# Sliding-window attention and MLP in one kernel: both halves of a block's scores in one run of matmuls, the second half in the PSUM banks that held an older block's values

## The chip, the cores and the metric

The kernel runs on one core of one Trainium2 chip. The metric is the device time of one launch in microseconds (us); lower is better. Times are given as the median of several runs, and everything that is read from a profile comes from one profiled execution.

## The reference

Two layers follow each other. The first is causal attention over a sliding window of 128 tokens, with a distance bias that differs by head (8 batches, 8 heads, 576 tokens, head size 64). The second is a layer norm with a gain, an MLP of 512 to 2048 to 512 with a ReLU, and a residual.

```python
scores = scale * np.matmul(q, k.transpose(0, 1, 3, 2))          # scale = 1/8
mask = (rel >= 0) & (rel < 128)                                 # rel = query - key
scores = np.where(mask, scores - slopes * np.abs(rel), -1e9)
attn = np.exp(scores - max); attn = attn / (sum + 1e-9)
x = np.matmul(attn, v)                                          # (8, 576, 512) after merging heads
xn = (x - mean) / sqrt(var + 1e-6) * g_ln
out = x + np.maximum(xn @ w_ch1, 0.0) @ w_ch2
```

The kernel leaves out the maximum: it takes exp(scale * scores) and multiplies it with exp(bias), which is zero outside the window.

## The kernel before, in words

**Blocks.** Batches are taken in pairs (p = 0 to 3). A pair has 9 blocks: blocks 0 to 7 hold 128 queries of one of the two batches, and block 8 (T) holds the last 64 tokens of both. That makes 36 blocks, numbered n = 9p + blk. An MLP group g takes 2 blocks (g = 0 to 3) or 4 blocks (g = 4 to 10).

**Attention of one block.** `attend` (L469) computes the scores of some heads with keys on the partitions: 64x64 tiles of the array, four of them beside each other (two halves of the keys by two heads). A block from 2 on has two halves of 4 heads each and so two calls of `attend`; a block 0 or 1 has one call with all 8 heads over its own keys, and T has two calls over the older keys and one (`tail_attend`) over its own. Each call issues 16 matmuls at L495 into one tile `ps_sc` of two PSUM banks, and one exp on ScalarE (L504) from there into `probs` in SBUF. `seen` (L443) lists which parts of the 64x128 score tiles can be seen through the window at all; from the ninth block on only those are computed (half of the matmuls have 64 columns, the others 128). `masks` (L513) multiplies `probs` by exp(bias) on VectorE (L516). `values_at_once` (L571) multiplies the weights with the values into the other tile, `ps_sc[0]` (matmuls at L579), and VectorE takes the result out with a reciprocal of the sums (L587) and a scaled copy (L588). `centre` (L602) subtracts the mean (L616, L620) and has the block turned by DMA. `square` (L661) computes the variance on ScalarE (L664).

**Steps.** For n from 8 on, a loop (L772 to L794) writes four steps for each n: the first has the loads, the values of block n, `centre`, and the first half of the scores of block n + 2; the second has the second half of these scores; the third has the mask of the first half, `square` and DMA transposes of later q and k; the fourth has the mask of the second half. Both halves go through `ps_sc[1]`, so `ps_sc[0]` is the values' alone. Where block n + 1 is a T, the two calls are T's own keys and the next pair's block 0 (n = 16, 25); for n = 8, 17, 26 and 34 there is one call alone. So 23 of the n have two calls.

**Order.** The order on all five engines is written by hand. `weave_at` (L1230) runs an MLP group's matmuls in units and, after unit u, emits the next steps whose place is u. The first MLP product (`mlp1`, L822) has 16 units of four 128x512 matmuls (L832) for a group of four blocks; each unit's ReLU goes to ScalarE (L848), and those of units 6 and 13 to VectorE (L840). The second (`mlp2_seven`, L1049) is a 2x2 block product in seven products instead of eight, each of 16 matmuls of 256 columns (L1062) and so four units, with an addition to the output on VectorE after each (L1083, two instructions). It needs sums of quarters of the hidden layer; `sum_hidden` (L1030, VectorE, L882) computes them during `mlp1` at the units of `SUMS_AT` (L48): after unit 11 three sums of parts 0 to 2 of each half, after unit 14 three of parts 3 to 5, after unit 15 three of parts 6 and 7. The sums after unit 11 need the ReLU of unit 10, those after unit 15 that of unit 15. Where both stand at one unit, the sums are emitted ahead of the steps.

The places of the steps stand in `TWICE` and `LEAD` (L795 to L797): for a group from g = 5 on, steps at units 4, 6, 8, 9 and 11, 13, 15, 15 of `mlp1`, and at 3, 7, 11, 15 and 19, 23, 27, 27 of `mlp2_seven`; g = 4 has 2, 4, 5, 6, then 7, 9, 9, 10, then 12, 14, 14 and, in `mlp2_seven`, 3 ahead of the eight others.

## Time and profile before

| | before |
|---|---|
| median of 3 runs | 308.04 us (307.87 to 308.59) |
| the profiled execution's own time | 307.95 us |
| its span in the profile | 306.2 us |
| granted TensorE clock, mean | 0.993 |
| busy: PE (matmuls) | 296.9 us |
| busy: DVE (VectorE) | 242.8 us |
| busy: ACT (ScalarE) | 181.7 us |
| busy: POOL (GpSimd, here only DMA issue) | 112.3 us |
| exps at L504, 128x1024 | 1.02 us each |
| masks at L516, 128x1024 | 0.68 us each |
| scaled copy of values at L588 | 0.69 us each |

The span is the time between the first and the last instruction of the profile; the 1.75 us between it and the execution's own time lie around it. Matmuls are pipelined, so the duration of one is longer than its share of the time: what counts is the distance between the starts. A row of the timeline gives the start, the time covered, the engine, the line, the shapes and, in brackets, for how long the engine sat idle before it and what ended that.

### The profile page before, as it was taken

To read this page: it belongs to the slowest core of one execution; us is meant where nothing else is said; L and a number is where in the kernel's file an instruction comes from. 1 tells how busy PE (TensorE), PEld (TensorE's weight loads), DVE (VectorE), ACT (ScalarE), POOL (GpSimd) and SP (SyncE) were. 2 spreads that over 40 slices of the span, in tenths; PEclk is the share of its full clock that TensorE was granted. 3 is DMA by queue.
4 is the path that set the end of the run, shared out by engine and by line. 5 is a ranking of instruction groups with operands and counts; after the bars stand their busy time and mean duration, and the time that the engine had idled before them with its cause. 6 is when DMAs were issued, how large, how long until landed. Compare 5 with 4: busy or idle time off the path is not lost.

```text
span 306.2 us, 9262 instructions
## 1 busy us (share of the span) xinstructions
PE 296.9 (97%) x3778; PEld 203.2 (66%) x3778; DVE 242.8 (79%) x646; ACT 181.7 (59%) x332; POOL 112.3 (37%) x153
## 2 busy tenths in 40 slices
PE   6899999999999999999999999999999999999994
PEld 2477755866755568646864686568656865698883
DVE  2588878779996799569967986798799878978983
ACT  5588776768966863675368635853586268506500
POOL 8933659763774372475107250760000000000000
PEclk9799999999999999999999999999999999999999
DMA  9999999999999999999999999999451043005014
GB/s 98 172 202 200 194 158 170 205 135 89 138 126 186 146 132 145 181 184 148 112 171 120 125 121 149 119 151 120 105 122 37 19 96 77 19 19 137 3 34 103
DMA packets 150074, 38.03 MB, mean 124 GB/s; under 512 B 140656, under 2 KB 145920, under 8 KB 150032
## 3 DMA queue, kind: packets, MB, share of 16 engines
q0 software_dynamic: 103792, 18.46, 96.0%
q1 hardware_dynamic: 45760, 18.60, 37.1%
q8 instruction: 29, 0.48, 0.7%
q10 hardware_dynamic: 480, 0.39, 0.5%
q14 instruction: 13, 0.11, 0.2%
HBM read 36.90 MB, written 9.44 MB: 151 GB/s over the span
## 4 chain that ended last, share of the span: by engine, by line
PE 91%; DMA 4%; ACT 1%; DVE 1%; POOL 1%; issue 1%; DVEq 0%; ACTq 0%; POOLq 0%
PE ps_m L832 35%; PE ps_s L1062 25%; PE ps_m L862 9%; PE ps_sc L495 6%; PE ps_sc L579 5%; PE ps_q L1141 4%; PE ps_x L956 3%; DMA q<-q 3%; DMA first<-in_k_dram 2%; PE ps_tr L343 1%; PE ps_warm L331 1%; POOL first L187 1%; PE ps_pv L550 1%; PE ps_tx L640 1%; PE ps_t L956 1%
## 5 line engine op out<-in xcount | busy, mean ns | idle before, releaser
L832 PE MATMUL ps_m<-xT,w1g 128*128 128x512 f16 (+1 forms) x512 | 103.7, 353 | 0.1
L848 ACT ACTIVATE ht_all<-ps_m 128x512 f16<-128x512 f32 (+1 forms) x143 | 71.5, 512 | 26.1 <-PE ps_m L832 24.0
L504 ACT ACTIVATE probs<-ps_sc 128x1024 f16<-128x1024 f32 x56 | 56.6, 1024 | 45.4 <-PE ps_sc L495 45.4
L832 PEld LDWEIGHTS <-w1g 128*128 128x128 f16 x512 | 47.7, 98 | 42.6 <-issue 0.3
L286 POOL DMA_DIRECT2D vx<-in_v_dram x40 | 34.1, 859 | 67.9 <-PE ps_sc L579 38.1
L1062 PE MATMUL ps_s<-w,s 128*128 128x256 f16 x384 | 43.8, 273 | 0.0
L1062 PEld LDWEIGHTS <-s 128*128 128x128 f16 x384 | 36.7, 98 | 4.7
L516 DVE TENSOR_TENSOR probs<-probs,m 128x1024 f16<-128x1024 f16 x56 | 36.9, 683 | 2.5 <-ACT probs L504 2.5
L1062 PE MATMUL ps_s<-w,ht_all 128*128 128x256 f16 x288 | 34.3, 273 | 0.0
L862 PE MATMUL ps_m<-w,ht_all 128*128 128x512 f16 x128 | 31.3, 380 | 0.0
L1062 PEld LDWEIGHTS <-ht_all 128*128 128x128 f16 x288 | 27.4, 98 | 4.9
L275 POOL DMA_DIRECT2D q<-in_q_dram x40 | 27.4, 697 | 6.0 <-DMA vx<-in_v_dram 2.2
L1083 DVE SCALAR_TENSOR_TENSOR o<-ps_s,rstd,x 128x256 f32<-128x256 f32 x48 | 21.0, 478 | 8.5 <-PE ps_s L1062 8.4
L882 DVE TENSOR_TENSOR s<-ht_all 128x1024 f16<-128x1024 f16 (+2 forms) x36 | 20.5, 571 | 7.9 <-ACT ht_all L848 6.7
L495 PE MATMUL ps_sc<-q,k 64*64 64x128 f16 (+1 forms) x1088 | 24.8, 212 | 0.6 <-ACT q L436 0.3
L495 PEld LDWEIGHTS <-k 64*64 64x64 f16 x1088 | 16.2, 108 | 13.2 <-issue 10.3
L588 DVE SCALAR_TENSOR_TENSOR x<-ps_sc,rec 128x512 f16<-128x512 f32 x32 | 22.1, 691 | 1.1
L272 POOL DMA_DIRECT2D k<-in_k_dram x20 | 17.9, 910 | 8.4 <-DMA k<-k 5.9
L664 ACT ACTIVATE junk<-xc 128x512 f16<-128x512 f16 x28 | 17.6, 628 | 5.7 <-DVE xc L620 5.6
L1083 DVE SCALAR_TENSOR_TENSOR o<-ps_s,rstd,o 128x256 f32<-128x256 f32 x36 | 15.7, 478 | 3.4 <-PE ps_s L1062 3.1
L579 PEld LDWEIGHTS <-probs 128*128 128x128 f16 x384 | 15.9, 98 | 3.6
L862 PEld LDWEIGHTS <-ht_all 128*128 128x128 f16 x128 | 11.1, 98 | 10.8
(117 smaller groups left out, 371.7 us busy)
## 6 DMA issues: line engine op xcount, KB each, us to landing
out_dram<-o SPq DMA_DIRECT2D x64, 128.0 KB, 2.5
vx<-in_v_dram POOLq DMA_DIRECT2D x32, 128.0 KB, 7.1
w<-in_moe_w_ch_dram POOLq DMA_DIRECT2D x8, 512.0 KB, 11.2
k<-in_k_dram POOLq DMA_DIRECT2D x30, 128.0 KB, 7.2
q<-in_q_dram POOLq DMA_DIRECT2D x48, 64.0 KB, 6.7
q<-in_q_dram POOLq DMA_DIRECT2D x10, 128.0 KB, 6.8
out_dram<-o SPq DMA_DIRECT2D x10, 64.0 KB, 1.9
k<-in_k_dram POOLq DMA_DIRECT2D x8, 64.0 KB, 7.7
```

Source lines behind the costliest of these rows:

```text
L275: nc.gpsimd.dma_start(out=t[half, b], in_=tokens.rearrange("h (c r) d -> r c h d", r=2)[r],)
L286: nc.gpsimd.dma_start(out=vx[p0 : p0 + n, :, 0:D], in_=v[b, :, t0 : t0 + n, :].rearrange("h p d -> p h d"),)
L495: nc.tensor.matmul(in_halves(ps[cols, j, n, t, :])[:, r, queries], kt[rows, hp, cols], in_halves(qt[rows, b, hp])[:, r, queries], start=no ...
L504: nc.scalar.activation(out=dst.rearrange("p (n j) q -> p j n q", j=2), in_=ps.rearrange("p j n t q -> p j n (t q)"), func=AF.Exp, scale=in ...
L516: nc.vector.tensor_tensor(out=dst, in0=dst, in1=mask, op=ALU.mult)
L579: nc.tensor.matmul(ps[:, h, 0 : D + 1], pr[:, h, t, :], vext[(p * NSLOT + o) % NV][:, h, :], start=(n == 0), stop=(n == len(terms) - 1),)
L588: nc.vector.scalar_tensor_tensor(out=x.rearrange("p (h d) -> p h d", h=H), in0=ps[:, :, 0:D], scalar=1.0, in1=rec.unsqueeze(2).broadcast_t ...
L832: nc.tensor.matmul(ps[:, 0:cols], w[:, kb, fb * P : (fb + 1) * P], xT[:, kb, 0:cols], start=(kb == 0), stop=(kb == NKB - 1),)
L848: nc.scalar.activation(out=ht[:, fb, :], in_=ps[:, 0:cols], func=AF.Relu)
L862: nc.tensor.matmul(sums[at], ht[:, fb, at * P : (at + 1) * P], w2[:, fb, :], start=(fb == 0), stop=(fb == NFB - 1),)
L1062: nc.tensor.matmul(ps[:, pair, :], lhs[:, fb, at : at + P], rhs[:, fb, :], start=(first and pair == 0 and fb == 0), stop=(fb == half - 1), ...
L1083: nc.vector.scalar_tensor_tensor(out=outs[at][:, cols], in0=ps[:, pair], scalar=rstd[:, n : n + 1], in1=(xs[p, blk] if fresh else outs[at] ...
```

## The change

The first half's `attend` moves from the first step into the second, so that the 32 matmuls of the two halves follow each other. The first half stays in `ps_sc[1]`; the second goes to `ps_sc[0]`, where the values of block n are. What lies there outside the visible parts is old, so `seen` gives the whole tiles for these calls. The second half's exp is not emitted with its matmuls but in the third step (`exps`), and both masks stand in the fourth. The places are changed: the third step comes at unit 7 instead of 8, 14 instead of 15, and 9 instead of 11, the fourth at 13 instead of 15; the second step of the last quarter at 22 instead of 23 and the third at 24 instead of 27.

```diff
-    def seen(p, blk, o, t):
+    def seen(p, blk, o, t, all_of_it):
...
-        if p == 0 and blk < SEEN:
+        if all_of_it or p == 0 and blk < SEEN:
             return [(0, both, every), (1, both, every)]
...
-    def attend(p, blk, keys, mask, tag, hps, sc=None):
+    def attend(p, blk, keys, mask, tag, hps, sc=None, put_off=False):
...
-                for c, r, queries in seen(p, blk, o, t):
+                for c, r, queries in seen(p, blk, o, t, sc == 0):
...
-        nc.scalar.activation(
-            out=dst.rearrange("p (n j) q -> p j n q", j=2),
-            in_=ps.rearrange("p j n t q -> p j n (t q)"),
-            func=AF.Exp,
-            scale=inv_sqrt_d,
-        )
+
+        def weights():
+            nc.scalar.activation(
+                out=dst.rearrange("p (n j) q -> p j n q", j=2),
+                in_=ps.rearrange("p j n t q -> p j n (t q)"),
+                func=AF.Exp,
+                scale=inv_sqrt_d,
+            )
+
+        if put_off:
+            scored_only.append(weights)
+        else:
+            weights()
...
+    def exps():
+
+        while scored_only:
+            scored_only.pop()()
...
         step += [(centre,) + order[n]]
-        step += [(attend, *args, 1) for args in todo[:1]]
-        second = [(attend, *args, 1) for args in todo[1:]]
-        third = [(masks, *args[:2], 1) for args in todo[:1]] + [(square, n)]
+
+        second = [(attend, *args, sc, sc == 0) for args, sc in zip(todo, (1, 0))]
+        third = [(exps,), (square, n)]
...
-        fourth = [(masks, *args[:2], 1) for args in todo[1:]]
+        fourth = [(masks, *args[:2], 1) for args in todo]
...
-    TWICE = [4, 6, 8, 9, 11, 13, 15, 15], [3, 7, 11, 15, 19, 23, 27, 27]
-    LEAD = [([2, 4, 5, 6, 7, 9, 9, 10, 12, 14, 14], [3] + TWICE[1])]
+    TWICE = [4, 6, 7, 9, 11, 13, 14, 15], [3, 7, 9, 13, 19, 22, 24, 27]
+    LEAD = [([2, 4, 5, 6, 7, 9, 9, 10, 12, 14, 15], [3] + TWICE[1])]
```

More of the change, by code (lines that the diff above doesn't have):

```diff
@@ L436, in copy_second @@
             copy(out=dst, in_=ps[b][:, 0 if t is q else 1])
-    weights_of, unmasked, scored = {}, {}, []
+    weights_of, unmasked, scored, scored_only = {}, {}, [], []
     def in_halves(t):
         return t if len(t.shape) == 3 else t.rearrange("p (r c) -> p r c", r=2)
-    def seen(p, blk, o, t):
+    def seen(p, blk, o, t, all_of_it):
         both, every = slice(0, 2), slice(0, HALF)
         first, second = slice(0, HALF // 2), slice(HALF // 2, HALF)
-        if p == 0 and blk < SEEN:
+        if all_of_it or p == 0 and blk < SEEN:
             return [(0, both, every), (1, both, every)]
```

## The prediction, as it was put on record

> **What bounds the kernel now.** I read the page's busy times first, then its chain of work that ended last, then the timelines of PE, DVE and ACT around the scores.

> ```profile
> PE 296.9 (97%) x3778; PEld 203.2 (66%) x3778; DVE 242.8 (79%) x646; ACT 181.7 (59%) x332; POOL 112.3 (37%) x153
> ```
> ```profile
> PE 91%; DMA 4%; ACT 1%; DVE 1%; POOL 1%; issue 1%; DVEq 0%; ACTq 0%; POOLq 0%
> ```

> PE is the bound. Between 95 and 262 us the timeline of PE shows no stall longer than about 0.12 us; whatever PE saves or waits there is saved or lost at the end. Even without stalls, something is lost around each call of `attend` ("a go"):

> ```profile
> 160.59 1.90 PE L832 MATMUL ps_m<-xT,w1g 128*128 128x512 f16 x8
> 162.42 0.37 PE L495 MATMUL ps_sc<-q,k 64*64 64x128 f16 x16
> 162.72 0.61 PE L832 MATMUL ps_m<-xT,w1g 128*128 128x512 f16 x2
> ```

> A unit of four L832 matmuls takes 0.862 us (the ReLUs at 156.45, 157.31, 158.18, 159.04 are that far apart). Eight from 160.59 are through at 162.31; the first score matmul starts 0.10 later; the next L832 starts at 162.72. So a go of 16 costs 0.40, about 0.10 of it on entering and 0.10 on leaving the 64x64 tiling.

> **What the change saves on PE.** A go of 16 with all columns, at 18.27, follows four 128x256 from 17.74 (to 18.17) and ends with the next L832 at 18.62: 0.45. One of 32 with all columns, at 52.92, follows eight 128x512 from 51.10 (to 52.82), and the next matmul comes at 53.49: 0.67. Two such goes in one save 0.23. Here two of 0.40 become 0.67 less the 0.05 that the first half saves by its fewer columns, 0.62: 0.18 saved, full columns of the second half paid for. 18 pairs of ordinary blocks save 0.177 each (3.2); three T pairs, whose halves cost 0.35 each and whose second half doubles its columns, 0.13 each (0.4); two pairs of a T's own keys and a block 0, 0.21 each (0.4). At 86.18 PE waits 0.2 for a transposed q (the chain shows DMA q<-q up to there); that go moves later and the wait ends. **Sum -4.2 us.** Exps, masks and DMAs are the same in number.

> **What it adds: a wait.** The second half writes `ps_sc[0]`, so its first matmul waits for L588 of block n, which takes the values out of it. All of PE's queue stands behind it. The question is whether L588 has ended by then. It does late in `mlp2_seven`, at unit 3 (group 6, DVE and then PE):

> ```profile
> 172.63 0.43 DVE L882 TENSOR_TENSOR s<-ht_all 128x512 f16<-128x512 f16 x1
> 173.09 0.42 DVE L882 TENSOR_TENSOR s<-s,ht_all 128x512 f16<-128x512 f16 x1
> 173.55 0.43 DVE L882 TENSOR_TENSOR s<-ht_all,s 128x512 f16<-128x512 f16 x1
> 173.89 1.29 DVE L516 TENSOR_TENSOR probs<-probs,m 128x1024 f16<-128x1024 f16 x2
> 175.10 0.87 DVE L1083 SCALAR_TENSOR_TENSOR o<-ps_s,rstd,x 128x256 f32<-128x256 f32 x2
> 175.88 0.20 DVE L587 RECIPROCAL rec<-ps_sc 128x8 f32<-128x8 f32 x1
> 176.11 0.69 DVE L588 SCALAR_TENSOR_TENSOR x<-ps_sc,rec 128x512 f16<-128x512 f32 x1
> ```
> ```profile
> 173.55 0.65 PE L579 MATMUL ps_sc<-vx,probs 128*128 128x65 f16 x16
> 174.13 0.37 PE L495 MATMUL ps_sc<-q,k 64*64 64x128 f16 x16
> 174.43 1.92 PE L1062 MATMUL ps_s<-w,ht_all 128*128 128x256 f16 x16
> 176.28 0.37 PE L495 MATMUL ps_sc<-q,k 64*64 64x128 f16 x16
> ```

> No idle time in brackets: DVE has worked without a gap since 167.0. The values' matmuls end at 174.04, L588 at 176.80. Before, nobody on PE cared; the second go started at 176.28. In the changed kernel it must not. [...]

> Let E be the end of L588 and S the start of the second go before. After the change the second half's matmuls start 0.18 before S (a go of 0.40 is gone from ahead of them, 0.22 of its matmuls are put back), 0.43 earlier still where its place is 22 and not 23. PE follows DVE by 0.06 (xc ends at 24.56, L640 starts at 24.62). From the timeline, all pairs with E + 0.06 later than that (E, S): n = 10 (83.09, 83.13), 15 (115.92, 114.44), 18 (138.82, 138.75), 19 (145.94, 145.04), 22 (169.60, 169.76), 23 (176.80, 176.28), 27 (207.31, 207.06), 28 (214.53, 215.12, at 22), 30 (231.39, 231.55), 31 (238.59, 238.07). The stalls are 0.20, 1.72, 0.31, 1.14, 0.08, 0.76, 0.49, 0.08, 0.08, 0.76: **5.6 us with nothing else moved.**

> **What else moves: ACT's order.** The ReLU on ACT is what the sums on DVE wait for. Before, after the second go of group 6:

> ```profile
> 170.19 1.02 ACT L504 ACTIVATE probs<-ps_sc 128x1024 f16<-128x1024 f32 x1 [0.59 <-PE ps_sc L495]
> 171.14 0.60 ACT L848 ACTIVATE ht_all<-ps_m 128x512 f16<-128x512 f32 x1
> 172.00 0.60 ACT L848 ACTIVATE ht_all<-ps_m 128x512 f16<-128x512 f32 x1 [0.27 <-PE ps_m L832]
> 172.50 0.62 ACT L664 ACTIVATE junk<-xc 128x512 f16<-128x512 f16 x1
> ```

> That is one exp, then ReLU 14, ReLU 15, then `square`. After: exp A, ReLU 14, exp B, `square`, ReLU 15. ACT takes the next instruction 0.94 after an exp's start, 0.50 after a ReLU's, 0.61 after a `square`'s. Group 6 from its first unit (times of before):
> - Units 4 to 6: pair 21, L588 at 161.33, no stall. Half A starts at 162.02, unit 7 at 162.54. Exp A 162.47, ReLU 7 163.61 (0.21 after its unit), exp B 164.10, `square` 165.05, ReLU 8 165.66, 9 166.15, 10 from 166.65 to 167.25. Before it ended at 166.98. So the sums, L587 and L588 of n = 22 are 0.27 later: E = 169.87.
> - Half B of n = 22 could start at 169.40 (S less 0.18, less 0.18 from pair 21): stall 0.53.
> - Unit 14 from 170.26 to 171.12, unit 15 to 171.98. ReLU 14 171.33, exp B 171.82, `square` 172.77, ReLU 15 from 173.38 to 173.98. The last three sums start at 174.0 and not 172.63: L588 of n = 23 ends 1.37 later, 178.17.
> - Half B of n = 23 could start at 176.28 - 0.18 - 0.35 + 0.53 = 176.28: stall 1.95.

> The same arithmetic for the others: n = 30 and 31 as 22 and 23 (0.53, 1.95). n = 18 has only one exp ahead (0.31); n = 19's ReLU 15 ends at 142.92, its sums start 1.18 late, E = 147.12 against 145.00: 2.18. n = 14: ReLU 10 comes behind both exps and `square`, ends at 106.36, not 105.93, E = 108.98 against 108.31: 0.73; n = 15: DVE is busy throughout, the same work 0.44 later, E = 116.36 against 114.48: 1.94. n = 27: E + 0.27 against 206.67: 0.97. n = 10: both masks now run ahead of L587 instead of one in a gap, E = 83.51 against 82.77: 0.80. n = 28: 0.10. **Stalls 12.0 us.**

> **Sum.** -4.2 + 12.0 = +7.8 on the profiled execution's 307.95 (its own time is within 0.1 of the median 308.04): 315.8 us.

> What I cost at nothing: exp B ahead of the next values in `ps_sc[0]` (group 6: ends at 172.8, values at 173.7; if late, PE waits as long). The later ReLU 15 against PE's own use of it in the second product (173.98 against 174.97; beyond that 1.0 every delay is PE's). SP's queue: some transposes of q and k go ahead of four stores; a store takes 2.5 to land and is not waited for before its buffer's next use. POOL's loads of v, which wait for L579, keep their places in the steps and move with PE.

> **The rivals.**
> - *Faster*: L588 is early enough, since PE's savings or a different DVE order remove the backlog. Only the gaps remain: 307.95 - 4.2 = 303.8. For it: in 12 of 23 pairs no stall is expected. Against it: at unit 3 of `mlp2_seven` L588 is already too late in five groups. From the end of the last sums to the end of L588 DVE works 2.8 (173.98 to 176.80 above), so for no stall at 176.28 the sums would have to end by 173.4, 1.4 after unit 15; ReLU 15 takes 0.8 of that at the least and the sums 1.3. Chance 0.07.
> - *Direct wait alone*: ACT's new order costs nothing, because DVE would have had the work in the same time: -4.2 + 5.6, 309.4. Against it: the last sums of group 6 start 0.03 after ReLU 15's end already before. Chance 0.2.
> - *The delay spreads*: ReLU 15 runs past the 1.0 of cover, PE waits a second time in four groups, about 1 us each: 320. Chance 0.1.
> - *The change does not do what it says*: 32 matmuls cost two goes all the same. Then nothing is gained on PE and 12 us of stalls stay: 320. The 0.67 at 52.92 speaks against it. Chance 0.03.
> - The forecast, 313 to 319: 0.6.

> A range from 309.2 to 320.2 takes in the direct wait alone at its lower and the delay that spreads at its upper end, and leaves out the first rival and the tails. Of no change I can tell from 0.2% (0.6 us) up: faster 0.07, same 0.03, slower 0.90.

> **What will show it.** Gaps: 23 goes of 32 with 0.62 around them. Waits: PE at the scores waiting for DVE at the scaled copy, some ten times, longest about 2 us, in `mlp2_seven` at unit 7. ReLU 15 behind a `square`, the last sums right behind it with idle time put down to ACT. Wrong would be: no wait of PE on that line (then the faster rival), waits that sum to 5 or 6 us (the direct wait alone), or stalls of PE at L1062 or L832.

## The result, and the profile after

| | before | after |
|---|---|---|
| median of 6 runs each, side by side | 308.08 us (307.58 to 308.59) | 318.87 us (315.11 to 321.25) |
| ratio | | 1.0324 (95%: 1.0273 to 1.0375) |
| the profiled execution's own time | 307.95 us | 315.11 us |
| its span | 306.2 us | 313.3 us |
| granted TensorE clock in it | 0.993 | 1.000 |

The forecast of 315.8 was a sum on the profiled execution; the profiled execution of the changed kernel took 315.11. Its median lies 3.8 above that and 3.1 above the forecast, though within the range, and why it does is a question of its own below. The slowest of the six was a disturbed run and is not in the ratio.

The busy times of the profile after:

```profile
PE 294.9 (94%) x3778; PEld 201.2 (64%) x3778; DVE 242.7 (77%) x646; ACT 180.4 (58%) x332; POOL 113.6 (36%) x153
```

There are as many instructions as before. PE is busy for 2.0 us less in a span that is 7.1 longer: it stands idle. The chain of work that ended last, by engine, tells for whom; before, PE had 91% of it, DVE and ACT 1% each:

```profile
PE 66%; DVE 14%; ACT 6%; DMA 5%; POOL 4%; issue 3%; DVEq 0%; POOLq 0%
```

From the view of waits (who waits <- for whom: us in total, times, longest), two lines. The first has no counterpart before. In the second, the sums of the hidden layer waiting for the ReLU, the total was 6.7:

```profile
PE ps_sc L495 <- DVE x L600: 9.9, 10, 2.0
DVE s L894 <- ACT ht_all L860: 11.2, 12, 1.3
```

(In the changed kernel the lines from the exp on are 2 and those from `masks` on 12 further down: L504 is L506, L516 is L528, L588 is L600, L848 is L860, L1062 is L1074.) How one of the long waits comes about is read from three timelines of group 6, around the values of n = 23. ACT:

```profile
174.43 0.60 ACT L860 ACTIVATE ht_all<-ps_m 128x512 f16<-128x512 f32 x1 [0.68 <-PE ps_m L844]
174.93 1.02 ACT L506 ACTIVATE probs<-ps_sc 128x1024 f16<-128x1024 f32 x1
175.83 0.63 ACT L676 ACTIVATE junk<-xc 128x512 f16<-128x512 f16 x1
...
176.44 0.60 ACT L860 ACTIVATE ht_all<-ps_m 128x512 f16<-128x512 f32 x1
```

That is ReLU 14, exp B, `square`, ReLU 15, without a gap. ReLU 15 ends at 177.04, and DVE has waited for it:

```profile
177.07 0.43 DVE L894 TENSOR_TENSOR s<-ht_all 128x512 f16<-128x512 f16 x1 [1.09 <-ACT ht_all L860]
...
178.33 1.29 DVE L528 TENSOR_TENSOR probs<-probs,m 128x1024 f16<-128x1024 f16 x2
179.54 0.87 DVE L1095 SCALAR_TENSOR_TENSOR o<-ps_s,rstd,x 128x256 f32<-128x256 f32 x2
180.32 0.20 DVE L599 RECIPROCAL rec<-ps_sc 128x8 f32<-128x8 f32 x1
180.56 0.69 DVE L600 SCALAR_TENSOR_TENSOR x<-ps_sc,rec 128x512 f16<-128x512 f32 x1
```

The scaled copy ends at 181.25, and 0.06 later PE goes on:

```profile
177.33 1.91 PE L1074 MATMUL ps_s<-w,ht_all 128*128 128x256 f16 x16
179.17 0.37 PE L495 MATMUL ps_sc<-q,k 64*64 64x128 f16 x16
181.31 0.42 PE L495 MATMUL ps_sc<-q,k 64*64 64x128 f16 x16 [1.77 <-DVE x L600]
181.66 0.61 PE L1074 MATMUL ps_s<-w,s 128*128 128x256 f16 x4
```

The first half's 16 matmuls stand at 179.17, the second half's at 181.31. Where nothing waits, the two halves' starts are 0.20 apart (165.14 and 165.34 in the same profile), so PE lost 1.94 here (the brackets count from the modelled end of the last matmul, 0.37 after 179.17, and show 1.77).

The distance between the two halves' starts, less 0.20 (0.15 at n = 15, where the scores are those of a T, as measured in the T pair at 188.80, which does not wait), gives the wait of every n in the same way:

| n | 10 | 14 | 15 | 18 | 19 | 22 | 23 | 27 | 28 | 30 | 31 | sum |
|---|---|---|---|---|---|---|---|---|---|---|---|---|
| forecast | .80 | .73 | 1.94 | .31 | 2.18 | .53 | 1.95 | .97 | .10 | .53 | 1.95 | 12.0 |
| of it, direct wait alone | .20 | 0 | 1.72 | .31 | 1.14 | .08 | .76 | .49 | .08 | .08 | .76 | 5.6 |
| after | .79 | .68 | 1.90 | .34 | 2.17 | .51 | 1.94 | .85 | .12 | .50 | 1.94 | 11.7 |

### The profile page after: what moved, and what is told of

Same layout as the page of the kernel before. It is cut to its first block, busy times and chain, and to the rows that moved or that the text cites. A ratio compares the mean times of both kernels' runs of the same rounds, so it can differ in the third digit from the quotient of the medians.

```text
span 313.3 us, 9275 instructions
## 1 busy us (share of the span) xinstructions
PE 294.9 (94%) x3778; PEld 201.2 (64%) x3778; DVE 242.7 (77%) x646; ACT 180.4 (58%) x332; POOL 113.6 (36%) x153
## 4 chain that ended last, share of the span: by engine, by line
PE 66%; DVE 14%; ACT 6%; DMA 5%; POOL 4%; issue 3%; DVEq 0%; POOLq 0%
PE ps_m L844 25%; PE ps_s L1074 18%; PE ps_m L874 7%; DVE s L894 5%; PE ps_sc L495 4%; PE ps_q L1153 4%; DMA w<-in_moe_w_ch_dram 3%; PE ps_x L968 3%; PE ps_sc L591 3%; DVE x L600 3%; ACT ht_all L860 2%; DVE probs L528 2%; ACT probs L506 2%; POOL vx L286 2%; DMA q<-in_q_dram 2%
## 5 line engine op out<-in xcount | busy, mean ns | idle before, releaser
L860 ACT ACTIVATE ht_all<-ps_m 128x512 f16<-128x512 f32 (+1 forms) x143 | 70.9, 511 | 30.1 <-PE ps_m L844 27.4
L506 ACT ACTIVATE probs<-ps_sc 128x1024 f16<-128x1024 f32 x56 | 55.9, 1022 | 50.7 <-PE ps_sc L495 50.7
L286 POOL DMA_DIRECT2D vx<-in_v_dram x40 | 35.2, 889 | 75.0 <-PE ps_sc L591 58.8
L1074 PE MATMUL ps_s<-w,s 128*128 128x256 f16 x384 | 44.6, 273 | 0.0
L1074 PEld LDWEIGHTS <-s 128*128 128x128 f16 x384 | 36.4, 98 | 5.0
L528 DVE TENSOR_TENSOR probs<-probs,m 128x1024 f16<-128x1024 f16 x56 | 36.2, 683 | 2.7 <-ACT probs L506 2.7
L1074 PE MATMUL ps_s<-w,ht_all 128*128 128x256 f16 x288 | 34.2, 273 | 0.0
L495 PE MATMUL ps_sc<-q,k 64*64 64x128 f16 (+1 forms) x1088 | 23.1, 213 | 10.7 <-DVE x L600 9.9
L495 PEld LDWEIGHTS <-k 64*64 64x64 f16 x1088 | 15.9, 107 | 24.0 <-issue 23.1
L1074 PEld LDWEIGHTS <-ht_all 128*128 128x128 f16 x288 | 27.8, 98 | 4.4
L894 DVE TENSOR_TENSOR s<-ht_all 128x1024 f16<-128x1024 f16 (+2 forms) x36 | 20.5, 570 | 12.1 <-ACT ht_all L860 11.2
L1095 DVE SCALAR_TENSOR_TENSOR o<-ps_s,rstd,x 128x256 f32<-128x256 f32 x48 | 20.9, 477 | 8.9 <-PE ps_s L1074 8.9
L600 DVE SCALAR_TENSOR_TENSOR x<-ps_sc,rec 128x512 f16<-128x512 f32 x32 | 22.1, 691 | 1.1
L1095 DVE SCALAR_TENSOR_TENSOR o<-ps_s,rstd,o 128x256 f32<-128x256 f32 x36 | 15.7, 478 | 6.6 <-PE ps_s L1074 6.6
## 6 DMA issues: line engine op xcount, KB each, us to landing
w<-in_moe_w_ch_dram POOLq DMA_DIRECT2D x8, 512.0 KB, 11.2
```

The costliest lines, as they stand in the source:

```text
L286: nc.gpsimd.dma_start(out=vx[p0 : p0 + n, :, 0:D], in_=v[b, :, t0 : t0 + n, :].rearrange("h p d -> p h d"),)
L495: nc.tensor.matmul(in_halves(ps[cols, j, n, t, :])[:, r, queries], kt[rows, hp, cols], in_halves(qt[rows, b, hp])[:, r, queries], start=no ...
L506: nc.scalar.activation(out=dst.rearrange("p (n j) q -> p j n q", j=2), in_=ps.rearrange("p j n t q -> p j n (t q)"), func=AF.Exp, scale=in ...
L528: nc.vector.tensor_tensor(out=dst, in0=dst, in1=mask, op=ALU.mult)
L600: nc.vector.scalar_tensor_tensor(out=x.rearrange("p (h d) -> p h d", h=H), in0=ps[:, :, 0:D], scalar=1.0, in1=rec.unsqueeze(2).broadcast_t ...
L860: nc.scalar.activation(out=ht[:, fb, :], in_=ps[:, 0:cols], func=AF.Relu)
```

## The experiments

**The theory**: what the change saves on PE is there, some 4.2 us; the waits of the second half for the scaled copy take it all and 7.5 more; a part of these waits comes from ACT's new order. **Rivals**: ACT's order costs nothing, since DVE is the late one anyway; the merged go saves less than worked out; the price lies in the full columns of the second half. A later question was why the median is above the profiled execution.

### ACT's order taken back

Only the step with the second half's exp and `square` goes back, in `mlp1`, to where the step with `square` was before, behind ReLU 8 and ReLU 15. The waits' cause, the shared banks, stays.

```diff
-    TWICE = [4, 6, 7, 9, 11, 13, 14, 15], [3, 7, 9, 13, 19, 22, 24, 27]
+    TWICE = [4, 6, 8, 9, 11, 13, 15, 15], [3, 7, 9, 13, 19, 22, 24, 27]
```

> The changed kernel with the third step of the first MLP product back at its old places (units 8 and 15 instead of 7 and 14), so that ScalarE has the ReLU of unit 15 ahead of the second exp and of square. Theory (ScalarE's new order delays ReLU 15, and with it the last sums and the scaled copy): the waits of PE at unit 7 of the second product shrink for n = 19 from 2.17 to 1.0, for n = 23 and 31 from 1.94 to about 0.85; those at unit 13 (n = 22, 30) grow from 0.50 to 0.9, since the second exp now stands behind ReLU 8 and pushes ReLU 10; n = 27 to 1.2. In sum 2.3 us less: 312.8 where the changed kernel's profiled execution has 315.1. Rival (VectorE's own backlog sets the wait, ScalarE's order has no part): no change, 315.1 at the same clock, waits within 0.1 of those of the changed kernel.

Median 315.25 us (4 runs), ratio 1.0225 (1.0171 to 1.0279). Its profiled execution took 313.34 at clock 1.000, 1.8 less than that of the changed kernel, also at 1.000. The line of the waits:

```profile
PE ps_sc L495 <- DVE x L600: 7.8, 10, 1.7
```

By the starts, n = 19, 23 and 31 wait 1.01, 0.78 and 0.78 instead of 2.17, 1.94 and 1.94. In return n = 22, 27 and 30 wait 0.88, 1.49 and 0.87 instead of 0.51, 0.85 and 0.50; the sum is 9.6, 2.1 less. So ACT's order is a part of the price and not all of it: at n = 23 the direct wait alone had been put at 0.76, and 0.78 is what was left. The three waits that grow do so by ACT's order as well. Exp B and `square` now run behind ReLU 8, at n = 22 some 0.9 later against the values' matmuls than in the changed kernel, and hold up ReLU 10, for which the sums after unit 11 wait. These sums start 0.74 after the start of the values' matmuls (168.72), where in the changed kernel it was 0.36:

```profile
169.46 0.56 DVE L894 TENSOR_TENSOR s<-ht_all 128x768 f16<-128x768 f16 x1 [0.89 <-ACT ht_all L860]
```

That 0.37 is what the wait of n = 22 gained, and that of n = 30. At n = 27, where 1.2 was expected, a subtraction of the mean on DVE (L632) also took 0.63 instead of 0.35.

### The go put later

The go of 32 moves to where the scaled copy has ended: unit 14 instead of 13 of `mlp1`, and 11 instead of 7, 23 for the last one, of `mlp2_seven`. The exps and masks follow about a place later. The shared banks and the full columns stay.

```diff
-    TWICE = [4, 6, 7, 9, 11, 13, 14, 15], [3, 7, 9, 13, 19, 22, 24, 27]
-    LEAD = [([2, 4, 5, 6, 7, 9, 9, 10, 12, 14, 15], [3] + TWICE[1])]
-    LEAD += 4 * [TWICE] + [(TWICE[0], [7, 11, 15, 19]), ([], [])]
+    TWICE = [4, 6, 7, 9, 11, 14, 15], [3, 3, 11, 13, 15, 19, 23, 25, 27]
+    LEAD = [([2, 4, 5, 6, 7, 9, 10, 10, 12, 15], [0, 3] + TWICE[1][1:])]
+    LEAD += 4 * [TWICE] + [(TWICE[0], [3, 7, 11, 15, 19]), ([], [])]
```

> The changed kernel with the merged go put off where it waited: one unit later in the first product (14 instead of 13; 15 instead of 14 in group 4) and four units later in the second (11 instead of 7), its last quarter at 23 again; exps and masks follow one place later each. Theory (each merged go saves 0.18 of PE, 4.2 in all, and the loss is only that its second half comes too early for the copy of the values): waits are left for n = 10 (0.8) and n = 15 (0.9), the others go; 307.95 - 4.2 + 1.7 = 305.5, faster than the kernel before. Rival (the merged go saves less than read off the gaps, or the wait moves along with it): 308 or more, waits of PE on the copy summing to over 4 us.

Median 306.77 us (10 runs), ratio 0.9968 (0.9944 to 0.9993), 1.3 above what the theory expected. One wait is left on the line, 0.6 in the view (0.79 by the starts), at n = 10, whose place the edit does not touch:

```profile
PE ps_sc L495 <- DVE x L600: 0.6, 1, 0.6
```

From the values of n = 9 to those of n = 34 PE is 2.4 us faster than before, with 1.6 us of waits still in that stretch (in group 4, 0.31 ahead of the values and 0.51 for an addition at L1095 that stands behind the sums, besides the 0.79 at n = 10): 4.0 saved without them, against the 4.2 of the forecast. That the merged go saves much less than worked out is out. The 1.3 lie outside that stretch: PE reaches n = 9 0.4 us later than before, and the values of n = 35 take 0.84 us longer, because PE waits for a mask (L528, 0.7 in the view).

### What was left, put right as well

In addition the go of n = 10 comes three units later in group 3, one step of group 4 comes a unit later, and three steps of group 9 come earlier. The edit is shown against the kernel with the go put later.

```diff
-    LEAD = [([2, 4, 5, 6, 7, 9, 10, 10, 12, 15], [0, 3] + TWICE[1][1:])]
-    LEAD += 4 * [TWICE] + [(TWICE[0], [3, 7, 11, 15, 19]), ([], [])]
+    LEAD = [([2, 4, 5, 6, 7, 9, 10, 11, 12, 15], [0, 3] + TWICE[1][1:])]
+    LEAD += 4 * [TWICE] + [(TWICE[0][:5] + [13, 14, 15], [7, 11, 15, 19]), ([], [])]
...
-            weave_at(mlp1(3, (9, 10, 11)), 4, 7, 8, 10, 12, 15, sums=0)
-            weave_at(mlp2(3), 0, 2, 3, 6, 9, 11, sums=4)
+            weave_at(mlp1(3, (9, 10, 11)), 4, 7, 8, 10, 12, sums=0)
+            weave_at(mlp2(3), 2, 2, 3, 5, 8, 9, 11, sums=4)
```

> As the kernel with the merged go put off, with three more places moved: the go of n = 10 three units later (the waits of 0.79 there), the masks of n = 13 a unit later (so that the sums of group 4 do not stand behind them), and group 9's second quarter back at 13, 14, 15 (n = 34 has no second half; its late mask held up the values of n = 35 by 0.85). Theory (4.2 us of PE saved, the rest is places): 306.8 - 0.8 - 0.8 - 0.5 = 304.7, 1.1% faster than the kernel before. Rival (these waits move to another place): 306 or more.

Median 305.6 us (6 runs), ratio 0.9909 (0.988 to 0.9938): 0.6 to 1.2% less than the kernel before. The median lies between the theory's 304.7 and the rival's 306, the profiled execution at 304.88. The line of PE waiting for the scaled copy is gone; by the starts 0.11 and 0.07 of such waits are left, at n = 11 and 15. Other waits are left or new, of which the longest are 0.36 ahead of the values of n = 11 and 0.30 ahead of those of n = 15; in sum it is 1.2. So a part of the waits did move, as the rival said. PE's timeline at n = 23 shows what a go of 32 costs when nothing waits:

```profile
172.52 1.91 PE L1074 MATMUL ps_s<-w,ht_all 128*128 128x256 f16 x16
174.27 1.91 PE L1074 MATMUL ps_s<-w,s 128*128 128x256 f16 x16
176.11 0.59 PE L495 MATMUL ps_sc<-q,k 64*64 64x128 f16 x32
176.64 3.67 PE L1074 MATMUL ps_s<-w,s 128*128 128x256 f16 x32
```

A product of 16 takes 1.75 (172.52 to 174.27), so that from 174.27 is through at 176.02; the next starts at 176.64. That is the 0.62 of the forecast.

### Two goes again where the waits are long

The old two goes, both into `ps_sc[1]`, return for n = 15, 19, 23, 27 and 31, whose waits make 8.8 of the 11.7. The other pairs and all places stay as changed.

```diff
+        if n in (15, 19, 23, 27, 31):
+            step += [(attend, *args, 1) for args in todo[:1]]
+            second = [(attend, *args, 1) for args in todo[1:]]
+        else:
-        second = [(attend, *args, sc, sc == 0) for args, sc in zip(todo, (1, 0))]
+            second = [(attend, *args, sc, sc == 0) for args, sc in zip(todo, (1, 0))]
```

> The changed kernel with the old two goes for n = 15, 19, 23, 27 and 31 alone (the values at unit 3 of the second product). Theory: their waits of 1.90, 2.17, 1.94, 0.85 and 1.94 go (8.8), five times 0.18 is lost again (0.9), the other waits (0.80, 0.68, 0.34, 0.51, 0.12, 0.50, in sum 2.9) stay: the changed kernel's 315.1 - 7.9 = 307.2 at a granted clock of 1, and since no wait is over 0.8 the granted clock does not fall within the execution, so that the median is within 1 of the profiled time. Rival (the time is lost in the later ReLU and sums, not in the wait of the second half): the second product still waits, 310 or more.

Median 309.88 us (10 runs), ratio 1.0041 (1.0019 to 1.0063): 2.7 above what the theory expected, and near the rival's. The waits of these five are gone (the line falls from 9.9 to 2.0), but PE now waits elsewhere. Lines here are 4 further down than in the changed kernel. In group 5, after the second half's go of n = 19, first PE and then DVE:

```profile
146.21 0.37 PE L495 MATMUL ps_sc<-q,k 64*64 64x128 f16 x16
147.32 1.47 PE L1078 MATMUL ps_s<-w,s 128*128 128x256 f16 x12 [0.74 <-DVE o L1099]
```
```profile
143.93 0.43 DVE L898 TENSOR_TENSOR s<-ht_all 128x512 f16<-128x512 f16 x1 [0.92 <-ACT ht_all L864]
...
146.40 0.87 DVE L1099 SCALAR_TENSOR_TENSOR o<-ps_s,rstd,x 128x256 f32<-128x256 f32 x2
```

The third product needs the bank of the first, which L1099 takes out; L1099 stands behind the masks and the sums, and the sums have waited for ReLU 15. From a go of 16 to the next L1078 it is 0.30 where nothing waits; here it is 1.11, and 0.89 at n = 23 and 31, so these waits are 0.81, 0.58 and 0.58. A fourth, 0.84, comes at the first unit of `mlp1` of group 5. In the changed kernel the wait for the scaled copy had covered them: DVE's lateness was paid once, at the first place that needed it. The sum can be compared with PE's way from the values of n = 9 to those of n = 34: -8.8 + 0.9 (five pairs' saving given up) + 2.0 + 0.84 = -5.1; measured -5.2. The profiled execution took 310.65, only 4.5 less than that of the changed kernel, because PE had reached n = 9 0.7 us later.

### Full columns alone

The kernel before, in which only the second half of each pair computes all columns.

```diff
-        second = [(attend, *args, 1) for args in todo[1:]]
+        second = [(attend, *args, 1, True) for args in todo[1:]]
```

> The kernel before with all columns computed in each second go, and nothing else changed: the part of the change that costs PE time by itself. Theory (18 goes 0.05 longer, three of T 0.10, two not at all): 308.1 + 1.2 = 309.3. Rival (the narrower matmuls are limited by their issue and not by their columns, so that full ones cost nothing): 308.1.

Median 310.18 us (12 runs), ratio 1.004 (1.0014 to 1.0066), 1.2 us. In the profile a second go takes 0.35 from its start to the next matmul instead of 0.30 in 18 pairs, 0.35 instead of 0.25 in the three of a T, and the same as before in two. That is 1.2, which the forecast had already taken off the saving; the price of the change does not lie there.

### The waits filled, and the changed kernel's spread

Why is the median of the changed kernel 3.8 above its profiled execution? The runs that listed a granted clock of about 0.988 took some 318.8, the one of 1.000 took 315.11. Theory: a long stand of PE takes away granted clock afterwards. Rival: the start of a run or the chip makes the spread. The edit fills the five long waits with matmuls into the scores' own banks, whose results do not count: half A overwrites the visible parts, and the mask makes the rest zero. The scaled copy ends no earlier, but PE does not stand.

```diff
+    def filler(n):
+        for _ in range(n):
+            nc.tensor.matmul(ps_sc[1][:, 0], iden, ones, start=True, stop=True)
...
+        second = [(filler, {15: 8, 19: 9, 23: 8, 27: 4, 31: 8}.get(n, 0))]
+        second += [(attend, *args, sc, sc == 0) for args, sc in zip(todo, (1, 0))]
```

> The changed kernel with matmuls of 512 columns that nobody reads put ahead of the first half of the scores where PE waited long (n = 15, 23, 31: 8; 19: 9; 27: 4), into the first half's own banks. PE works there instead of waiting, so the work ends no sooner: profiled 315 to 315.5 at a granted clock of 1.0. Theory on the 3.8 us between the changed kernel's profiled execution (315.1 at clock 1.000) and its median (318.9 at 0.988): PE's stands of about 2 us sometimes lower the granted clock afterwards; filled, the runs show 0.992 or more and a median of 315 to 316.5. Rival (the clock falls for a reason that has nothing to do with these waits): the median stays at 318 to 319 with a clock of 0.988.

> The changed kernel as it is, once more, beside the others on the same chip. Both theories on the clock: a median near 318.9 with clocks of about 0.988. The theory that PE's waits lower the clock expects a profiled execution with a clock under 1 to show the low stretches within some us after a wait of about 2 us; the rival expects them elsewhere.

Filled: median 315.8 us (4 runs: 315.77, 315.77, 315.83, 318.07). The changed kernel beside it: median 318.6, one of its runs at 315.83, four from 318.15 to 318.89, the profiled one at 321.61. The filled kernel's profiled execution is the one of 318.07, where 315 to 315.5 had been expected. Its trace has the clock at half from 8.31 to 15.14 and at full from there to 315.5: the start makes a part of the spread, as the rival has it. Both kernels ran again:

> The kernel with filled waits, again, for its spread: the same waits of PE ahead of the second halves at n = 15, 19, 23, 27, 31, but filled with matmuls into the scores' own banks that nobody reads. Theory (stands of PE of about 2 us take away granted clock for one stretch afterwards, and that is what lifts the median of the changed kernel from the 315.1 of its profiled execution to 318.7): with nothing standing there the executions lie near 315.8, a median of 315.6 to 316.4. Rival (the start, or the chip, makes the spread, whatever PE does in the middle): the median lies as high as that of the changed kernel beside it, 318 or more.

> The changed kernel itself beside it, for its spread. Theory: most executions between 318 and 319, at a granted clock of 0.988 or so, and few near 315; a median of 318.3 to 319, some 2.5 above the filled kernel. Rival: the same median as the filled kernel within 0.8.

Filled: median 316.33 us, 316.1 to 317.04 (6 runs). Not filled: 319.88, 319.08 to 320.33 (6 runs). The two do not overlap, and the kernel with 37 more matmuls is 3.5 us faster, where 2.5 had been expected. Where the time goes is seen in the changed kernel's profile of these last runs (319.94 us, clock 0.983), in stretches of 3.4 us around three of its four long waits. The columns: the stretch; its length, then the busy time of PE, PEld, DVE, ACT and POOL with the number of instructions; the granted clock; DMA:

```profile
112.90:116.30 3.40, 1.67 (x42) 1.19 (x40) 3.29 (x10) 1.27 (x2) 0.88 (x1) 0.99 2.12 125
116.30:119.70 3.40, 3.40 (x19) 2.44 (x17) 0.95 (x3) 1.39 (x3) 0.00 (x0) 0.51 1.81 151
...
181.20:184.60 3.40, 1.63 (x33) 1.21 (x34) 3.32 (x9) 1.02 (x1) 3.40 (x6) 1.00 1.04 72
184.60:188.00 3.40, 3.40 (x45) 2.99 (x45) 2.36 (x7) 1.63 (x3) 1.82 (x2) 1.00 1.48 106
245.90:249.30 3.40, 1.64 (x42) 1.17 (x40) 3.30 (x10) 1.33 (x2) 0.00 (x0) 1.00 0.01 2
249.30:252.70 3.40, 3.40 (x18) 2.43 (x17) 1.12 (x4) 1.32 (x3) 0.00 (x0) 0.50 0.40 43
```

In the first, second and last pair PE was busy for 1.6 to 1.7 of 3.4 us, because it waited 1.90, 1.94 and 1.94. After the first and the last the clock is 0.5 for 3.4 us, and PE gets through 18 or 19 matmuls where it does 45. The same happens at 150.4, after the wait of 2.16. Half the clock for 3.4 us is 1.7 us lost; three of them, 5.1, off 319.94 give 314.8, about the 315.11 of the execution at full clock. After the wait at n = 23, just as long, nothing happens, and in the first profile of the changed kernel none of the four waits had such a stretch behind it. The profile of 321.61 repeats it: half the clock for 3.4 us from 118.05, 152.18 and 251.17, after the same three waits and not after that of n = 23, and once at the start, from 8.8; less four times 1.7, 314.8 is left here as well. So a stand of some 2 us does this sometimes; what decides was not tried. The mean clock that is listed does not order all runs either (one of 319.81 has 0.995), so that the accounting holds for these two profiles, and for the other runs only the difference of 3.5.

## Why the prediction was right

- **PE bounds, and what it waits is lost at the end**: right. -4.2 + 11.7 = +7.5. The profiled executions differ by 7.16. The one after had no stretch of half clock at the start (that before had one, 8.1 to 11.5) and was about 0.7 ahead by n = 9. From the values of n = 9 to those of n = 34, where the change acts, PE is 7.75 slower; with the 4.0 of the next point the sum is +7.7.
- **The saving, -4.2**: right to 0.2; 4.0 where the waits are gone, and 0.62 for a go of 32 to the hundredth. The full columns cost what was taken off for them, 1.2.
- **The direct wait**: right in place and mechanism. Every n that was named waits, none that was not, and the longest is at unit 7 of `mlp2_seven`.
- **ACT's order**: right. Each of the eleven waits was forecast within 0.12, the sum within 0.3. With the exp back behind ReLU 15, what remains at n = 23 is the direct wait's 0.76 to 0.02.
- **What was costed at nothing**: in the changed kernel neither the third product nor the next values waited for more. But the claim that the later ReLU 15 is covered was about PE's own use of it, and left out the other one: the sums also hold up L1099, which frees a bank for the third product. It cost nothing after only since PE was waiting already; with the two goes back it cost 2.0.
- **The shared banks**: writing the second half where the values' reader still was cost 11.7 us of waits here. The kernel with the go put later shows the other side: the same reuse of the banks costs next to nothing once the reader has been through them (0.07 at n = 15 instead of 1.90, nothing at n = 19, 23, 27 and 31).
- **The rivals**: *faster* would have needed no waits on that line; there are ten in the view. *Direct wait alone* is refuted by the 11.2 us of sums waiting for the ReLU and by ACT's order taken back. *The delay spreads* did not happen here and was there under the first wait, as the two goes showed. *Does not do what it says* falls with the 0.62.
- **What is missing in the sum**: the granted clock after a long stand, 3.5 us in the median. The forecast met the profiled execution, which had none of it: that was luck, and so was it that the median lies in the range, whose upper end stood for another delay. The term could have been asked for: before, PE stood for 0.9 us in all between 20 and 300 us, so no row of it could price a stand of 2 us.

## What to carry to other kernels

When an engine's next instruction writes where another engine still reads, all that is queued behind it stands as well (PE for up to 2.17 us here). Do not ask whether the buffer is free on average: work out when the reader ends, with everything queued ahead of it, and compare that with the writer's start. The remedy may be the place and not the buffer: the same 32 matmuls one to four units later turned +3.2% into -0.3%, and with the remaining waits cleared into -0.9%. And before taking a long wait away, look for a second, shorter one that it hides: removing 8.8 us of waits here uncovered 2.8.

## What the runs showed of the hardware

Behind six of the twelve waits of PE of 1.90 to 2.18 us, four in each of the three profiles of the changed kernel, the granted clock was half for one stretch of 3.4 us: 1.7 us lost, nearly as much again as the wait. Behind stands of up to 0.8 us after the first 20 us no such stretch was seen in the two kernels with the go put later: the clock from 20 to 300 us was 1.00 in both.

The waits with and without half the clock behind them lie differently on that grid. The six with it ended 0.48 to 1.01 us before the end of their stretch of the grid. Of the six without, five ended at most 0.35 before such an end or behind it, and one had begun 0.4 before its stretch (the grid of the first profile, which has no half clock until its end, is counted on from 6.76). How busy PE was in the stretch does not tell them apart: 1.41 to 1.68 us with half the clock behind it, and 1.64 from 242.28 to 245.69 in the first profile, with the full clock behind it. This is read from twelve waits; no run shifts a wait on the grid, so that its place decides is not shown.
